# The key-value state of a linear attention block: one product of unrounded operands, or three of rounded parts

## The chip, the cores and the metric

The kernel runs on one core of one Trainium2 chip. The time is the device time of one execution in microseconds (us). Five engines matter: TensorE (PE; its weight loads are listed apart as PEld), VectorE (DVE), ScalarE (ACT), GpSimd (POOL), and SyncE (SP), which issues all DMAs here. Each engine works through its own instructions in the order in which they stand.

## The reference

One block on x of 2048 tokens by 576 columns, all float32. x is layer-normalized; then a linear attention with 32 heads of 18 columns and a gated feed-forward net (576 to 4608 to 576) are multiplied.

```python
q, k, v = qkv[0], qkv[1], qkv[2]
phi = lambda t: jnp.where(t > 0, t + 1, jnp.exp(t)) + 1e-6      # elu + 1
pq, pk = phi(q), phi(k)
kv = jnp.einsum("bhsd,bhse->bhde", pk, v)
z = jnp.einsum("bhsd->bhd", pk)
num = jnp.einsum("bhqd,bhde->bhqe", pq, kv)
den = jnp.einsum("bhqd,bhd->bhq", pq, z)[..., None] + 1e-6
o = num / den
...
s = _A_ref(xn, A_wqkv, A_wo)
g = _silu(_B_ref(xn, B_w1, B_b1, B_w2, B_b2))
return x + s * g
```

The change concerns `kv` and `z`, called the state below: sums over all tokens of value times key, and of the keys.

## The kernel before, in words

Most products on TensorE are made of rounded parts. A float32 operand is split into a high part, rounded to the type `F32R` by a copy (listed as CAST), and a low part, the difference, rounded to the same type; the product is then high·high + high·low + low·high, three products of rounded operands in place of one of unrounded ones. The state was an exception: its operands were plain float32, and each of its products was one instruction in the program.

The first stage (to about 149 us of the span) goes over 16 tiles of 128 tokens, t = 0 to 15. For each tile:

- x of the tile is made ready, transposed and split into `xh` and `xl`. Tiles 0 to 3 are normalized in rows (for 1 to 3 on ScalarE, `normalize_x`, L221), transposed on TensorE (`transpose_x`, bank `pt`) and split from the bank (L238 to L249). From tile 4 on a transposed x is loaded, centred on POOL (L276), scaled on VectorE (L279), rounded on ScalarE (L287), and the rest subtracted on VectorE (L291, L292).
- TensorE projects keys and 126 columns of values into a PSUM tile of two banks, `pk`; later the other 450 value columns into `pv`. Both come from one pool of three such tiles.
- `phi` (L339) makes elu of the keys: relu, exp and a shift on ScalarE (L328, L330, L332, tile `e`), then one VectorE instruction (L334) that reads `pk` and `e` and writes the tile `phi` in SBUF. That was the last read of the keys in `pk`.
- `copy_v` (L364) copies the values on ScalarE (L367, L369) into one of two buffers `vb`, five groups of 126 columns or fewer, each with a column of ones behind, which gives `z`.
- `state` (L373) multiplies, for the tile before, each group of values (127 columns, the weights) with the same group of keys (126 columns, in the last group 72) and adds up in two banks, `ps_kva` and `ps_kvb`, over all tiles.

So the order on TensorE is: keys of t, (transposes of x tile t+1, up to t = 2), state of t−1, values of t. The state of tile 15 stands behind the first query projection. The whole stage is recorded with a helper that holds every engine to the order of the code, so an instruction that waits holds up all behind it on its engine. In the same queues stand the statistics of later x tiles (VectorE L190 to L194) and the splits of weights for the later stages (L392 to L431). The later stages (queries, attention output, up and down projections) take the rest of the span and are not changed.

At the start POOL clears the value buffers (L149) and puts in the ones (L150), between the steps that make the identity matrix for the warm-up transposes.

Of the kernel before, what the change touches and what calls it, by code (L numbers as in the profile page):

```python
# [8 lines left out]
F32 = mybir.dt.float32  # L9
F32R = mybir.dt.float32r  # L10
U8 = mybir.dt.uint8
AF = mybir.ActivationFunctionType
ALU = mybir.AluOpType
PSUM = bass.MemoryType.PSUM

P = 128
S = 2048
D = 576
HD = 288
# [3 lines left out]
NT = S // P  # L23
# [8 lines left out]
G = 7 * DH  # L32
GROUPS = [(g, min(G, D - g)) for g in range(0, D, G)]
NG = len(GROUPS)
# [10 lines left out]
def linear_attention_gated_ffn(ctx, tc, x, xT, wqkv, wo, w1, w1e, b1, w2, b2, out):  # L45
    nc = tc.nc
    SUB, MUL, ADD = ALU.subtract, ALU.mult, ALU.add
# [34 lines left out]
    def bank2(name):  # L82
        return psum.tile([P, 2, 512], F32, tag="pp", name=name)
# [4 lines left out]
    def as2(ap):  # L88
        return ap.rearrange("p (a b) -> p a b", a=2)
# [49 lines left out]
    t1 = ph1.enter_context(tc.tile_pool(name="t1", bufs=2, side="right", reuse_waits="tile"))  # L139
    nhalf = t1.tile([P, 1], F32, name="nhalf", bufs=1)  # L140
    nc.gpsimd.memset(nhalf, -0.5)
    tiny = cst.tile([P, 1], F32, name="tiny")
# [1 line left out]

    v_bufs = [t1.tile([P, NG, P], F32, name=f"vb{i}", bufs=1) for i in range(2)]
    for v in v_bufs:
        nc.gpsimd.memset(v, 0.0)  # L149
        nc.gpsimd.memset(v[:, :, G : G + 1], 1.0)  # L150

    mask = t1.tile([P, 4 * G], U8, name="mask", bufs=1)
    mf = t1.tile([P, 7, DH], F32, name="mf", bufs=1)
# [185 lines left out]
    def phi(pool, ps, name, between=lambda: None):  # L339
        out = []  # L340
        steps = phi_steps(pool, ps, name, out)
        next(steps)
        between()
        for _ in steps:
            pass
        return out
# [17 lines left out]
    def copy_v(v, g, ps):  # L364

        n = ps.shape[1] // G
        nc.scalar.copy(v[:, g : g + n, :G], ps[:, : n * G].rearrange("p (g c) -> p g c", c=G))  # L367
        if n * G < ps.shape[1]:
            nc.scalar.copy(v[:, g + n, : ps.shape[1] - n * G], ps[:, n * G :])  # L369

    ps_kv = []

    def state(t, k_t, v_t):  # L373
        for i, (g, n) in enumerate(GROUPS):
            dst = ps_kv[0][: G + 1, g : g + n] if i < 4 else ps_kv[1][: G + 1, :n]
            nc.tensor.matmul(  # L376
                dst, v_t[:, i, : G + 1], k_t[:, g : g + n],
                start=(t == 0 and i in (0, 4)), stop=(t == NT - 1), skip_group_check=True,
            )

# [137 lines left out]
    for t in range(NT):  # L520
# [19 lines left out]
        pk = bank2(f"pk{t}")  # L540
        v_t = v_bufs[t % 2]
# [17 lines left out]
        values = lambda: copy_v(v_t, 0, pk[:, 1, HD : HD + VB])  # L559
        if t + 1 < NTR:  # L560
            if t:
                k_t, _ = phi(t1, pk, f"k{t}", values)
            transpose_x(t + 1)
            if t == 0:
                project(t, wv_h, wv_l, pv, FIRST_V[1], cols=v_cols, begin=False)
            for j in sums2:
                w2_hi(j)
            for j in sums2:
                w2_lo(j)
            if t - 1 in WE_SUMS:  # L570
                we_hi(WE_SUMS[t - 1]), we_lo(WE_SUMS[t - 1])
            if t == 0:
                layernorm(2)
            if t + 2 < NTR:
                offset(t + 2)
            if t == 0:
                k_t, _ = phi(t1, pk, f"k{t}")
        else:
            if not last:
                set_x_hi(t + 1), set_x_lo(t + 1)  # L580
            for j in sums2:
                w2_hi(j)
            for j in sums2:
                w2_lo(j)
            if t - 1 in WE_SUMS:
                we_hi(WE_SUMS[t - 1]), we_lo(WE_SUMS[t - 1])
            k_t, _ = phi(t1, pk, f"k{t}", values)
        if pend is not None:
            if not ps_kv:
                ps_kv += [bank1("ps_kva"), bank1("ps_kvb")]  # L590
# [515 lines left out]
    for i in range(1, NT + 4):  # L1106
        if 2 < i < NT:
            query(i)
        if i in X_STORES:
            at, src = X_STORES[i]  # L1110
# [461 lines left out]
    for step in range(n_chunks):  # L1572
        half, c = divmod(step, NC)
# [77 lines left out]
        for j in range(CF // 2):  # L1651
            n = 2 * step + j
# [64 lines left out]
```

## Time and profile before

| | us |
|---|---|
| median of 3 runs | 1093.29 (1093.01 to 1093.33) |
| the profiled execution, its own time | 1093.08 |
| span of its instructions | 1091.2 |
| of the span, first stage to the end of the last state | about 149 |
| busy in the first 45 to 60 us: PE, DVE, ACT, POOL (of 15) | 15.00, 12.12, 7.80, 9.86 |
| granted TensorE clock over the span | 1.00 |

In a row of the timeline stand the start, the duration, the engine, the line, the operation, the output and inputs, sizes, and in brackets how long the engine stood idle before it and what ended the wait. In a row of groups stand the count, the busy time, the mean in ns of one instruction, and the idle time before them. A product of two unrounded float32 operands appears as two records on PE and on PEld; one of rounded parts as one.

### The profile page before, as it was taken

To read this page: it belongs to the slowest core of one execution; us is meant where nothing else is said; L and a number is where in the kernel's file an instruction comes from. 1 tells how busy PE (TensorE), PEld (TensorE's weight loads), DVE (VectorE), ACT (ScalarE), POOL (GpSimd) and SP (SyncE) were. 2 spreads that over 40 slices of the span, in tenths; PEclk is the share of its full clock that TensorE was granted. 3 is DMA by queue.
4 is the path that set the end of the run, shared out by engine and by line. 5 is a ranking of instruction groups with operands and counts; after the bars stand their busy time and mean duration, and the time that the engine had idled before them with its cause. 6 is when DMAs were issued, how large, how long until landed. Compare 5 with 4: busy or idle time off the path is not lost.

```text
span 1091.2 us, 18129 instructions
## 1 busy us (share of the span) xinstructions
PE 1083.6 (99%) x6710; PEld 1007.8 (92%) x6710; DVE 794.9 (73%) x1100; ACT 548.8 (50%) x957; POOL 456.6 (42%) x391
## 2 busy tenths in 40 slices
PE   9999999999999999999999999999999999999998
PEld 8999999999898998988989989899898998988988
DVE  7766459888688898888988988657475574664856
ACT  6545466465646456465564654624335244252552
POOL 3566414332546455464555553414324143241340
PEclk9999999999999999999999999999999999999999
DMA  7997635675958658576585669968676666767352
GB/s 239 240 226 210 215 103 182 213 246 183 342 221 315 219 195 331 172 292 235 205 332 176 261 232 409 379 234 309 223 231 215 213 225 225 229 220 226 126 185 87
DMA packets 87106, 254.28 MB, mean 233 GB/s; under 512 B 11751, under 2 KB 24039, under 8 KB 84330
## 3 DMA queue, kind: packets, MB, share of 16 engines
q1 hardware_dynamic: 87018, 253.13, 68.9%
q8 instruction: 53, 0.87, 0.3%
q14 instruction: 35, 0.29, 0.1%
HBM read 156.57 MB, written 94.58 MB: 230 GB/s over the span
## 4 chain that ended last, share of the span: by engine, by line
PE 99%; DMA 0%; DVE 0%; SPq 0%; issue 0%; ACT 0%
PE pm L1349 35%; PE a L1187 16%; PE e L1187 10%; PE bc L1187 10%; PE pk L315 6%; PE pq L315 6%; PE ps_s L811 5%; PE pv L315 4%; PE pd L1465 2%; PE ps_kva L376 1%; PE ptp L793 1%; DMA w<-wqkv 0%; PE ps_kw L725 0%; PE ps_kvb L376 0%; SPq L353 0%
## 5 line engine op out<-in xcount | busy, mean ns | idle before, releaser
L1355 DVE TENSOR_TENSOR macc<-pm,macc 128x576 f32<-128x576 f32 x218 | 164.2, 753 | 56.3 <-PE pm L1349 55.8
L835 ACT CAST h_h<-g 128x512 fp32r<-128x512 f32 x204 | 122.7, 620 | 132.6 <-PE pm L1349 132.0
L838 DVE TENSOR_TENSOR h_l<-g,h_h 128x512 fp32r<-128x512 f32 x204 | 154.6, 768 | 14.8 <-ACT h_h L835 13.9
L1315 POOL TENSOR_TENSOR mid<-g 128x512 f32<-128x512 f32 x34 | 43.9, 1292 | 130.2 <-ACT g L1203 130.2
L1216 ACT COPY mid<-a 128x512 f32<-128x512 f32 x36 | 21.1, 587 | 110.5 <-PE a L1187 110.2
L1222 DVE TENSOR_TENSOR bc<-bc,mid 128x512 f32<-128x512 f32 x36 | 25.1, 697 | 52.2 <-PE bc L1187 40.7
L881 POOL TENSOR_TENSOR w1raw<-w1raw 128x256 f32<-128x256 f32 x18 | 13.2, 736 | 114.2 <-ACT h_h L835 65.6
L1309 POOL TENSOR_TENSOR g<-g 128x512 f32<-128x512 f32 x34 | 52.3, 1538 | 20.8 <-ACT h_h L835 16.7
L1235 DVE TENSOR_TENSOR z<-a,mid 128x512 f32<-128x512 f32 x36 | 25.1, 697 | 46.6 <-PE a L1187 46.6
L1437 POOL TENSOR_TENSOR fin1l<-fin1h,fin1l 128x288 f32<-128x288 f32 x8 | 7.1, 882 | 120.2 <-DMA fin1l<-s_dram 71.5
L1312 POOL TENSOR_TENSOR g<-g 128x512 f32<-128x512 f32 x34 | 52.5, 1545 | 7.6 <-DVE h_l L838 5.6
L1306 POOL TENSOR_TENSOR g<-g 128x512 f32<-128x512 f32 x34 | 50.4, 1482 | 2.7
L776 POOL TENSOR_TENSOR pbuf<-phiq,den 128x576 f32<-128x576 f32 x16 | 19.0, 1188 | 62.0 <-DVE den L775 62.0
L1225 ACT COPY mid<-a 128x512 f32<-128x512 f32 x36 | 21.1, 585 | 44.4 <-PE a L1187 44.3
L1236 ACT COPY mid<-a 128x512 f32<-128x512 f32 x36 | 21.1, 587 | 40.0 <-DVE z L1235 40.0
L838 DVE TENSOR_TENSOR h_l<-mid,h_h 128x512 fp32r<-128x512 f32 x34 | 38.1, 1120 | 2.0 <-ACT h_h L835 2.0
L315 PE MATMUL pk<-wkv_h,xh 128*128 128x288 f32 (+1 forms) x160 | 38.2, 321 | 0.5 <-DVE xh L245 0.5
L315 PE MATMUL pk<-wkv_l,xh 128*128 128x288 f32 (+1 forms) x160 | 38.5, 322 | 0.1
L811 PE MATMUL ps_s<-kw_h,th 128*128 128x288 f32 x160 | 35.3, 302 | 0.0
L315 PE MATMUL pq<-wq_h,xh 128*128 128x288 f32 x160 | 34.7, 298 | 0.0
L315 PE MATMUL pq<-wq_l,xh 128*128 128x288 f32 x160 | 34.3, 296 | 0.0
L763 POOL TENSOR_TENSOR eq<-phiq,zb 128x576 f32<-128x576 f32 x16 | 22.9, 1428 | 27.2 <-DVE kw L736 19.4
(891 smaller groups left out, 3709.5 us busy)
## 6 DMA issues: line engine op xcount, KB each, us to landing
we<-we_dram SPq DMA_DIRECT2D x36, 448.0 KB, 5.5
w2raw<-w SPq DMA_DIRECT2D x10, 1152.0 KB
w1raw<-w SPq DMA_DIRECT2D x18, 512.0 KB, 4.8
op_a<-wa SPq DMA_DIRECT2D x18, 512.0 KB, 4.7
op_c<-wc SPq DMA_DIRECT2D x18, 512.0 KB
op_d<-wd SPq DMA_DIRECT2D x18, 512.0 KB, 2.9
wc<-op_c SPq DMA_DIRECT2D x18, 512.0 KB, 6.7
wa<-op_a SPq DMA_DIRECT2D x18, 512.0 KB, 4.5
```

The costliest lines, as they stand in the source:

```text
L315: nc.tensor.matmul(ps[:, h, : ws.stop - ws.start], st, w[:, k, ws], start=(begin and i == 0), stop=(end and i == len(seq) - 1), skip_group ...
L811: nc.tensor.matmul(ps[:, h, :HD], st[:, k, :], w[:, k, h * HD : (h + 1) * HD], start=(i == 0), stop=(i == len(seq) - 1),)
L835: nc.scalar.copy(pair[0], src)
L838: eng.tensor_tensor(pair[1], src, pair[0].bitcast(F32), op=SUB)
L1187: nc.tensor.matmul(ps, st, mv, start=first and n == 0, stop=n == len(seq) - 1, skip_group_check=True,)
L1222: tt(B, B, m1_sb, op=ADD)
L1306: tt(src[5, pr], A(1, 0), A(1, 1), op=ADD)
L1309: tt(src[6, pr], src[5, pr], A(0, 0), op=SUB)
L1312: tt(src[3, pr], A(0, 1), src[6, pr], op=SUB)
L1315: tt(src[7, pr], A(0, 0), A(1, 0), op=SUB)
L1349: nc.tensor.matmul(ps[:, q, :HD], hs[p][st][:, cs], m[:, p, :], start=(n == 0 and i not in CHAIN), stop=(n == 5), skip_group_check=True,)
L1355: nc.vector.tensor_tensor(dst, src, dst, op=ADD)
```

## The change

Values and keys get a high and a low part, and the state becomes three products per group.

- The value buffers hold two parts, `[P, 2, NG, P]` in place of `[P, NG, P]`. `copy_v` rounds the values on ScalarE into part 0 and then subtracts on VectorE into part 1, reading the bank again. The ones are in part 0 and zeros in part 1.
- `phi_key` takes the place of `phi` for the keys. VectorE writes elu back into `pk`, in place; ScalarE rounds it from there into part 0 of a new tile `kk`, and VectorE subtracts part 0 from the bank into part 1.
- `state` runs fifteen products a tile, high·high, high·low and low·high for each of five groups.

Per tile that is one more ScalarE instruction (the cast of the keys), and on VectorE one subtraction for the keys and three for the values. No instruction is taken away, and no DMA is changed.

```diff
-    v_bufs = [t1.tile([P, NG, P], F32, name=f"vb{i}", bufs=1) for i in range(2)]
+    v_bufs = [t1.tile([P, 2, NG, P], F32R, name=f"vb{i}", bufs=1) for i in range(2)]
     for v in v_bufs:
-        nc.gpsimd.memset(v, 0.0)
-        nc.gpsimd.memset(v[:, :, G : G + 1], 1.0)
+        nc.gpsimd.memset(v.bitcast(F32), 0.0)
+        nc.gpsimd.memset(v[:, 0, :, G : G + 1].bitcast(F32), 1.0)
...
     def copy_v(v, g, ps):
         n = ps.shape[1] // G
-        nc.scalar.copy(v[:, g : g + n, :G], ps[:, : n * G].rearrange("p (g c) -> p g c", c=G))
+        parts = [(v[:, :, g : g + n, :G], ps[:, : n * G].rearrange("p (g c) -> p g c", c=G))]
         if n * G < ps.shape[1]:
-            nc.scalar.copy(v[:, g + n, : ps.shape[1] - n * G], ps[:, n * G :])
+            parts.append((v[:, :, g + n, : ps.shape[1] - n * G], ps[:, n * G :]))
+        for dst, src in parts:
+            nc.scalar.copy(dst[:, 0], src)
+        for dst, src in parts:
+            nc.vector.tensor_tensor(dst[:, 1], src, dst[:, 0].bitcast(F32), op=SUB)
+
+    def phi_key(ps, name, between=lambda: None):
+        e = t1.tile([P, D], F32, tag="e", name=f"e{name}")
+        kk = t1.tile([P, 2, D], F32R, tag="kk", name=f"kk{name}")
+        src = ps[:, :, :HD]
+        nc.scalar.activation(as2(e), src, AF.Relu, scale=-1.0)
+        between()
+        nc.scalar.activation(e, e, AF.Exp, scale=-1.0)
+        nc.scalar.activation(e, e, AF.Identity, bias=tiny[:, 0:1])
+        nc.vector.scalar_tensor_tensor(src, src, 1.000001, as2(e), op0=ADD, op1=ALU.max)
+        nc.scalar.copy(as2(kk[:, 0]), src)
+        nc.vector.tensor_tensor(as2(kk[:, 1]), src, as2(kk[:, 0]).bitcast(F32), op=SUB)
+        return kk
...
     def state(t, k_t, v_t):
         for i, (g, n) in enumerate(GROUPS):
             dst = ps_kv[0][: G + 1, g : g + n] if i < 4 else ps_kv[1][: G + 1, :n]
-            nc.tensor.matmul(
-                dst, v_t[:, i, : G + 1], k_t[:, g : g + n],
-                start=(t == 0 and i in (0, 4)), stop=(t == NT - 1), skip_group_check=True,
-            )
+            for j, (a, b) in enumerate(((0, 0), (0, 1), (1, 0))):
+                nc.tensor.matmul(
+                    dst, v_t[:, a, i, : G + 1], k_t[:, b, g : g + n],
+                    start=(t == 0 and i in (0, 4) and j == 0), stop=(t == NT - 1 and j == 2),
+                    skip_group_check=True,
+                )
...
-                k_t, _ = phi(t1, pk, f"k{t}", values)
+                k_t = phi_key(pk, f"k{t}", values)
```

The last replacement stands in all three places where the stage calls `phi` for keys; in tile 0 `phi` and now `phi_key` stand without `values`, whose copies come from `pv` later.

The new instructions stand in two queues at places where others wait. First ScalarE in tile 0, from the transposed x tile 1 (`pt1b`) to the first activation of tile 1's keys; `ek` is the tile `e` of the keys, `vb` a value buffer, `xn` the normalized x tile 2, `kkk` the tile `kk`. Before:

```order
L242 CAST xh_82<-pt1b 128x128
L328 ACTIVATE ek_307<-pk_216 128x576
L330 ACTIVATE ek_307<-ek_307 128x576
L332 ACTIVATE ek_307<-ek_307,tiny 128x576
L367 COPY vb_115<-pv_259 128x3x126
L367 COPY vb_115<-pv_259 128x126
L369 COPY vb_115<-pv_259 128x72
L221 ACTIVATE xn_316<-x_199,mv_302 128x576
L221 ACTIVATE xn_316<-x_199,mv_302 128x64
```

and now, with the engines that each instruction waits for:

```order
L242 CAST xh_82<-pt1b 128x128 [waits PE_49]
L380 ACTIVATE ek_307<-pk_216 128x576
L382 ACTIVATE ek_307<-ek_307 128x576 [waits Activation_49]
L383 ACTIVATE ek_307<-ek_307,tiny 128x576 [waits Activation_49]
L385 CAST kkk_308<-pk_216 128x576 [waits DVE_49]
L371 CAST vb_115<-pv_259 128x3x126 [waits PE_49]
L371 CAST vb_115<-pv_259 128x126 [waits DVE_49]
L371 CAST vb_115<-pv_259 128x72
L221 ACTIVATE xn_321<-x_199,mv_302 128x576 [waits DMAHW5_49,Pool_49]
L221 ACTIVATE xn_321<-x_199,mv_302 128x64
```

The cast of the keys, which waits for VectorE, is now ahead of the values' copies and of the normalization of x tile 2, and the second copy waits for VectorE too.

Second VectorE in a tile of the steady part, tile 4: from the scaling of x tile 5 (`xt`) to the statistics of a later one. Before:

```order
L279 TENSOR_TENSOR xt_441<-xt_441,bc_443 128x640
L291 TENSOR_TENSOR xl_85<-xt_441,xh_84 128x4x128
L292 TENSOR_TENSOR xh_84<-xt_441,xh_84 64x128
L431 TENSOR_TENSOR w1h<-w1u,w1h 128x896
L334 SCALAR_TENSOR_TENSOR phik_681<-pk_642,ek_676 128x576
L190 BN_STATS st_714<-x_536 128x6
```

and now:

```order
L279 TENSOR_TENSOR xt_461<-xt_461,bc_463 128x640 [waits DMAHW6_49,DMAHW5_49,Pool_49]
L291 TENSOR_TENSOR xl_85<-xt_461,xh_84 128x4x128 [waits Activation_49]
L292 TENSOR_TENSOR xh_84<-xt_461,xh_84 64x128
L451 TENSOR_TENSOR w1h<-w1u,w1h 128x896 [waits DMAHW1_49,Activation_49]
L373 TENSOR_TENSOR vb_115<-pk_692,vb_115 128x126 [waits PE_49,Activation_49]
L384 SCALAR_TENSOR_TENSOR pk_692<-pk_692,ek_726 128x2x288 [waits DVE_49,Activation_49]
L386 TENSOR_TENSOR kkk_727<-pk_692,kkk_727 128x576 [waits Activation_49]
L373 TENSOR_TENSOR vb_115<-pv_751,vb_115 128x3x126 [waits PE_49,Activation_49]
L373 TENSOR_TENSOR vb_115<-pv_751,vb_115 128x72
L190 BN_STATS st_779<-x_571 128x6 [waits DMAHW3_49]
```

The elu instruction has a value subtraction ahead of it and three subtractions behind it, of which the first waits for the cast of the keys and the second for the values of `pv`; the statistics and the scaling of the next x tile come after them.

More of the change, by code (lines that the diff above doesn't have):

```diff
@@ L576, in linear_attention_gated_ffn @@
             if t == 0:
-                k_t, _ = phi(t1, pk, f"k{t}")
+                k_t = phi_key(pk, f"k{t}")
         else:
@@ L586, in linear_attention_gated_ffn @@
                 we_hi(WE_SUMS[t - 1]), we_lo(WE_SUMS[t - 1])
-            k_t, _ = phi(t1, pk, f"k{t}", values)
+            k_t = phi_key(pk, f"k{t}", values)
         if pend is not None:
```

## The prediction

> **What bounds the kernel now.** I read the page's busy shares and its chain of waits first, then the timeline of TensorE around one token tile of the first stage, where the change lies.
>
> ```profile
> span 1091.2 us, 18129 instructions
> PE 1083.6 (99%) x6710; PEld 1007.8 (92%) x6710; DVE 794.9 (73%) x1100; ACT 548.8 (50%) x957; POOL 456.6 (42%) x391
> PE 99%; DMA 0%; DVE 0%; SPq 0%; issue 0%; ACT 0%
> ```
>
> TensorE is busy for 99% of the span and holds 99% of the chain that ended last: what TensorE is given more or less, the kernel gains or loses in full, and other engines matter only where they make it stand. The next view is the timeline of TensorE over tiles 3 and 4 of the first stage (start, duration, engine, line, operation, count).
>
> ```profile
> 39.18 1.05 PE L376 MATMUL ps_kva<-phik,vb 128*127 128x126 f32 x8
> 40.06 0.34 PE L376 MATMUL ps_kvb<-phik,vb 128*127 128x72 f32 x2
> 40.20 0.45 PE L315 MATMUL pv<-wkv_h,xh 128*128 128x450 f32 x1
> 40.49 0.36 PE L315 MATMUL pv<-wkv_l,xh 128*128 128x450 f32 x1
> 40.70 0.37 PE L315 MATMUL pv<-wkv_h,xl 128*128 128x450 f32 x1
> 43.16 0.48 PE L315 MATMUL pk<-wkv_h,xh 128*128 128x288 f32 x2
> 47.63 1.04 PE L376 MATMUL ps_kva<-phik,vb 128*127 128x126 f32 x8
> ```
>
> No row has an idle time in brackets: TensorE goes from state to values to keys without a stop, one tile every 47.63 − 39.18 = 8.45 us. A five-product state stands as ten records, since each product of unrounded operands is two, each with its own weight load. Its share: from 39.18 to the second pv product at 40.49, less one pv product (40.70 − 40.49 = 0.21), is 1.10 us, so 0.11 us a record. The 72-column records are no cheaper: (40.49 − 0.21 − 40.06) / 2 = 0.11. [...]
>
> **The change, part by part.**
>
> *State products on TensorE.* Five products of two records become fifteen products of rounded operands. Are those one record, and at which pace? The last down-projection has the narrowest rounded products of the trace in a row:
>
> ```profile
> 1085.14 0.50 PE L1465 MATMUL pd<-w__11186,hp 128*128 128x192 f32 x3
> 1085.47 0.50 PE L1465 MATMUL pd<-w__11206,hp 128*128 128x192 f32 x3
> 1085.81 0.50 PE L1465 MATMUL pd<-w__11222,hp 128*128 128x192 f32 x3
> ```
>
> Three products (one record each) take 0.33 to 0.34 us, 0.11 us each, though at the pace of the 450-column products (0.21 us, so 0.46 ns a column) 192 columns would need 0.09. [...] So a state takes 15 × 0.111 = 1.66 us in place of 1.10: +0.55 us, times 16 tiles = **+8.9 us**. Bounds: if only streaming counted, 126 and 72 columns need 0.057 and 0.033 us, a state 3 × (4 × 0.057 + 0.033) = 0.79 us, or −5.0 us in all; if each product took 0.115, +10.0 us. I take 0.111, which two kinds of row give.
>
> [...]
>
> *The keys in tiles 0 and 1.* What is new on ScalarE and VectorE is a queue order. ScalarE rounds the keys (cast) only after VectorE has written elu back to the bank; everything behind that cast on ScalarE waits. Here are the rows of ScalarE, VectorE and TensorE there, before:
>
> ```profile
> 17.98 0.78 ACT L332 ACTIVATE ek<-ek,tiny 128x576 f32<-128x576 f32 x1
> 18.67 0.62 ACT L367 COPY vb<-pv 128x378 f32<-128x378 f32 x2
> 19.18 0.23 ACT L369 COPY vb<-pv 128x72 f32<-128x72 f32 x1
> 19.70 1.20 ACT L221 ACTIVATE xn<-x,mv 128x576 f32<-128x576 f32 x2 [0.29 <-DVE mv L209]
> 23.45 0.67 ACT L238 CAST xh<-pt 128x640 fp32r<-128x640 f32 x1
> ...
> 19.69 0.76 DVE L334 SCALAR_TENSOR_TENSOR phik<-pk,ek 128x576 f32<-128x576 f32 x1
> 23.85 0.76 DVE L334 SCALAR_TENSOR_TENSOR phik<-pk,ek 128x576 f32<-128x576 f32 x1
> ...
> 21.15 0.71 PE L232 MATMUL pt<-ident,xn 128*128 128x128 f32 x5
> 25.67 0.49 PE L315 MATMUL pk<-wkv_h,xh 128*128 128x288 f32 x2
> ```
>
> and the prices of the new operations, from the groups by shape of the first 165 us:
>
> ```profile
> L334 DVE SCALAR_TENSOR_TENSOR phik<-pk,ek 128x576 f32<-128x576 f32 x16 | 12.1, 757 | 25.2 <-ACT ek L332 25.2
> L734 ACT COPY kw<-ps_kw 126x576 f32<-126x576 f32 x2 | 1.3, 639 | 1.5 <-PE ps_kw L725 1.5
> L246 DVE TENSOR_TENSOR xl<-pt,xh 128x512 fp32r<-128x512 f32 x2 | 1.4, 680 | 0.0
> L246 DVE TENSOR_TENSOR xl<-pt0a,xh 128x256 fp32r<-128x256 f32 x2 | 0.8, 424 | 0.1
> ```
>
> A cast of the keys is 0.64 us on ScalarE (a copy of the same size out of PSUM), the keys' subtraction 0.76 us on VectorE (its 576-column operation with one operand in PSUM), and the values' subtractions, at 1 ns a column and 0.17 us fixed (from 680 and 424), 0.55, 0.29 and 0.24 us for 378, 126 and 72 columns. Writing elu into PSUM instead of SBUF has no row; I take the same 757 ns, and bound it by 0 and +0.3.
>
> Tile 0, step by step: elu of keys 0 ends at 19.69 + 0.76 = 20.45. Cast: to 21.1. ScalarE's copy of the first 378 value columns: to 21.5. VectorE subtracts keys to 21.9, then those values to 22.4, and ScalarE's next copy (126 columns) waits for that subtraction, as its row in the order shows: to 22.7, the 72 columns to 22.9. Only then comes the normalization of x tile 2 (before at 19.70, 1.20 us for its two pieces), to about 24.0. TensorE wants it for the transposes at 21.15, and can start them on the first piece at about 23.65: **+2.5 us**, nothing else being ahead of them on TensorE. The state of tile 0, the values and the keys behind them go down by the same. The range is 1.8 (elu 0 earlier, no hand-off times) to 3.3 (each of seven hand-offs 0.1 dearer).
>
> Tile 1: VectorE's three statistics took from 20.45 to 23.85, 3.4 us with the hand-offs; now they begin at about 23.2, end at 26.7, elu of keys 1 ends at 27.7 (its value subtraction of 0.29 first), the cast at 28.35, and the cast of x tile 2 (0.67, before at 23.45), which now stands behind it, at 29.0. The keys of tile 2 want it at 25.67 + 2.5 + 0.55 = 28.7, so TensorE waits **+0.4 us** (bounds 0 and 1). The x tile after it, the last that ScalarE normalizes, has room: VectorE stood 4 us before the elu of keys 2, which the same delays fill first.
>
> ```profile
> 32.59 0.76 DVE L334 SCALAR_TENSOR_TENSOR phik<-pk,ek 128x576 f32<-128x576 f32 x1 [4.09 <-ACT ek L332]
> ```
>
> *VectorE in the later tiles.* New there: 0.76 for keys, 1.08 for values, and a wait of about 0.74 for the key cast; less 0.08 for each overlap at a start, 2.24 us a tile. The heaviest tile of the trace:
>
> ```profile
> 44.89:52.58 7.69, 7.69 (x50) 7.45 (x49) 6.77 (x10) 4.33 (x8) 4.45 (x3) 1.00 0.96 216
> 77.27:85.72 8.45, 8.45 (x54) 8.21 (x53) 6.25 (x11) 4.43 (x9) 6.54 (x6) 1.00 1.03 244
> ...
> 46.51 1.73 DVE L291 TENSOR_TENSOR xl<-xt,xh 128x512 fp32r<-128x512 f32 x1 [0.79 <-ACT xh L287]
> 83.84 0.76 DVE L334 SCALAR_TENSOR_TENSOR phik<-pk,ek 128x576 f32<-128x576 f32 x1 [1.25 <-ACT ek L332]
> ```
>
> From one scaling of x to the next (third column of busy times is VectorE) it needs 7.69 us with one wait of 0.79 for ScalarE's rounding of x, and 9.93 with the new work, against a TensorE tile of 8.45 + 0.55 = 9.00: it falls 0.9 us behind. The second window, without its wait of 1.25, comes to 7.2 + 2.24 = 9.44. Lighter tiles give it back. What it may lose: a value subtraction must end before the state one key projection later.
>
> ```profile
> 43.35 0.48 ACT L367 COPY vb<-pv 128x378 f32<-128x378 f32 x1 [0.91 <-PE pv L315]
> 43.72 0.23 ACT L369 COPY vb<-pv 128x72 f32<-128x72 f32 x1
> ```
>
> The copies end at 43.95, the subtractions 0.79 later at 44.7, the state comes at 47.63: 2.9 us of cover. I count **0**; with the cover gone, each of the ten tiles 3 to 12 costs 0.9, less the 2.9 of cover, +6 us at most.
>
> *The start.* POOL clears twice the width of the value buffers, 0.63 us more before the identity that the warm-up transposes need. They and the first keys come up to 0.6 us later, but the value weights behind them wait for DMA anyway:
>
> ```profile
> 1.00 0.63 POOL L149 MEMSET vb<- 128x640 f32 x1
> 2.02 4.03 PE L363 MATMUL warm<-ident 128*128 128x128 f32 x20 [2.02 <-POOL ident masks.py:199]
> 10.72 3.69 ACT L357 CAST wkv_h<-raw_v 128x576 fp32r<-128x576 f32 x5 [0.84 <-DMA raw_v<-wqkv]
> ```
>
> I count 0 (bounds 0 and 0.6). The sum: +8.9 + 2.5 + 0.4 = +11.8 us, on the profiled execution's 1093.08 (span 1091.2): 1104.9. The median of the runs is 0.2 above that execution, so I forecast **1105.1 us**.
>
> **The rivals.**
> (a) *VectorE becomes the bound.* The 9.93 against 9.00 repeats over the middle tiles and the cover is used up: +11.8 plus up to 6, 1107 to 1111, say 1109. For it speak the two windows above; against it VectorE's idle times before L334, 25.2 us over the sixteen tiles.
> (b) *Weights load ahead.* With a fifteen-long run of narrow loads the pace falls halfway between streaming (0.053 on average) and 0.111, 0.082 us: a state 1.23 us, +2.1 us in all, with +2.9 for the start 1098.1. The rows of 192 columns, twelve in a run, speak against it. [...]
> (c) *Faster.* Loads hidden wholly, 0.79 us a state: −5.0 + 2.9 = −2.1, 1091. It decides below a pace of (1.10 − 2.9 / 16) / 15 = 0.061 us a product. Even then VectorE's 9.93 would hold a tile above 8.45 for a while. Nothing in the rows reaches that pace.
> (d) *The change does not do what it says:* products of rounded parts below some width between 126 and 192 columns cost two records too. Thirty records of 0.111 are 3.33 us a state: +35.6 + 2.9, 1131.8.
> (e) *No stop at the start:* the normalization comes in time after all, +8.9 alone, 1102.
>
> **How the numbers follow.** Forecast 0.60, (a) 0.22, (b) 0.05, (c) 0.03, (d) 0.02, (e) 0.08. The range takes in (e), most of (a), and the bounds of the load price (+8.0 at 0.1075 us to +10.0) with those of the start: 1100 to 1112. A measurement of this kernel tells about 0.2%, 2.2 us, from no change. Faster by that needs less than 1091.1, (c) at its end: 0.02. Within it the rest of (c) and a little of (b): 0.03. Slower: 0.95.
>
> **What would show it.** In the changed profile a state should be fifteen records, 1.66 us from its first start to the values' start less their first lead; TensorE should show one idle time of about 2 us before the transposes of tile 2, released by ScalarE's normalization at L221, and under 0.5 before the keys of tile 2; no state should wait on VectorE's subtractions. The forecast is wrong if the products' starts stand 0.06 or 0.08 us apart, or if states in the middle tiles wait for VectorE.

## The result, and the profile after

| | before | changed |
|---|---|---|
| median, us | 1093.15 (1092.89 to 1093.33, 4 runs) | 1112.59 (1111.43 to 1113.17, 4 runs) |
| the profiled execution, its own time | 1093.08 | 1111.43 |
| span of its instructions | 1091.2 | 1109.3 |

The ratio is 1.0177, with a 95% interval of 1.0163 to 1.019: the kernel is slower by 19.4 us. I had forecast 1105.1, and the range to 1112 just misses the median. The profiled execution is the shortest of the four, with a mean granted clock of 0.998; the other three show 0.995, which matters further down.

First the page's head and its chain of waits:

```profile
span 1109.3 us, 18400 instructions
PE 1095.5 (99%) x6790; PEld 1018.1 (92%) x6790; DVE 824.5 (74%) x1164; ACT 557.3 (50%) x973; POOL 459.1 (41%) x391
PE 90%; DVE 5%; issue 2%; DMA 2%; ACT 1%; SPq 0%; POOL 0%; DVEq 0%
```

TensorE has 80 records more (16 tiles of 15 in place of 10) and 11.9 us more of busy time. But it now holds 90% of the chain where it held 99%: VectorE has 5%. The waits of TensorE, by what ended them (us in total, times, longest), say where:

```profile
PE warm L363 <- POOL ident masks.py:199: 2.5, 1, 2.5
PE pt L232 <- ACT xn L221: 2.3, 1, 2.3
PE ps_kva L395 <- ACT kkk L385: 1.6, 2, 1.4
PE ps_kva L395 <- DVE kkk L386: 1.3, 3, 0.5
PE pk L315 <- DVE kkk L386: 0.5, 1, 0.5
PE pk L315 <- DVE xh L245: 0.5, 1, 0.5
```

The first row is the wait for the identity matrix, 2.0 us before the change. The second and the fifth row are the two stops at the start, where the forecast has them. The third and fourth, 2.9 us of the state waiting for the keys' cast and subtraction, should not be there. The timeline of TensorE shows both, and between them a state in a tile without a stop:

```profile
24.03 0.77 PE L232 MATMUL pt<-ident,xn 128*128 128x128 f32 x5 [2.31 <-ACT xn L221]
29.85 0.55 PE L315 MATMUL pk<-wkv_h,xh 128*128 128x288 f32 x2 [0.52 <-DVE kkk L386]
...
52.98 1.44 PE L395 MATMUL ps_kva<-kkk,vb 128*127 128x126 f32 x12
54.26 0.47 PE L395 MATMUL ps_kvb<-kkk,vb 128*127 128x72 f32 x3
54.56 0.45 PE L315 MATMUL pv<-wkv_h,xh 128*128 128x450 f32 x1
54.84 0.36 PE L315 MATMUL pv<-wkv_l,xh 128*128 128x450 f32 x1
...
80.02 0.22 PE L395 MATMUL ps_kva<-kkk,vb 128*127 128x126 f32 x1
80.63 1.45 PE L395 MATMUL ps_kva<-kkk,vb 128*127 128x126 f32 x11 [0.39 <-DVE kkk L386]
89.66 1.44 PE L395 MATMUL ps_kva<-kkk,vb 128*127 128x126 f32 x12
108.83 1.44 PE L395 MATMUL ps_kva<-kkk,vb 128*127 128x126 f32 x12
119.43 0.33 PE L395 MATMUL ps_kva<-kkk,vb 128*127 128x126 f32 x1 [1.44 <-ACT kkk L385]
```

The state from 52.98 to 54.84, less one value product of 0.21, takes 1.65 us: 15 × 0.110. From tile 2 to tile 6 the states begin 9.01 us apart, as forecast. From the state of tile 6 on (80.02, then 89.66, 99.00, 108.83, 119.43 and 130.80) they come late: 9.64, 9.34, 9.83, 10.60 and 11.37 us apart, 5.73 more than five times 9.01, and then 9.01 again, from tile 11 on, where no statistics of later x tiles are left to make.

In the last of these steps there is something else as well. This is a window of 3.41 us in it (busy times of PE, PEld, DVE, ACT and POOL; the third number from the end is the granted TensorE clock):

```profile
122.14:125.55 3.41, 3.41 (x11) 3.02 (x10) 2.41 (x3) 3.20 (x6) 1.65 (x1) 0.50 0.48 164
```

TensorE had half its clock there, shortly behind a stop of 1.44 us ahead of the state and one of 0.47 behind its first product. Of the kernel before, the profiled execution shows none of this: its clock is 1.00 from 5.40 to 1090.84 us, all but the first and the last microseconds.

So there are two candidates for what the forecast left out, VectorE in the middle tiles and the clock, and in the median they make up some 7 us between them.

### The profile page after: what moved, and what is told of

The parts are those of the page before. It is cut to its first block, busy times and chain, and to the rows that moved or that the text cites. A ratio compares the mean times of both kernels' runs of the same rounds, so it can differ in the third digit from the quotient of the medians.

```text
span 1109.3 us, 18400 instructions
## 1 busy us (share of the span) xinstructions
PE 1095.5 (99%) x6790; PEld 1018.1 (92%) x6790; DVE 824.5 (74%) x1164; ACT 557.3 (50%) x973; POOL 459.1 (41%) x391
## 4 chain that ended last, share of the span: by engine, by line
PE 90%; DVE 5%; issue 2%; DMA 2%; ACT 1%; SPq 0%; POOL 0%; DVEq 0%
PE pm L1369 34%; PE a L1207 16%; PE bc L1207 10%; PE e L1207 10%; PE pq L315 5%; PE ps_s L831 5%; PE pd L1485 2%; PE pk L315 2%; PE pv L315 2%; PE ptp L813 1%; PE ps_kva L395 1%; DVE xh L292 1%; DVE pk L384 1%; DVE vb L373 1%; DMA x<-x 1%
## 5 line engine op out<-in xcount | busy, mean ns | idle before, releaser
L195 POOL TENSOR_TENSOR mv<-mv,nhalf 128x1 f32<-128x1 f32 x16 | 13.7, 854 | 53.3 <-DVE mv L194 53.3
```

## The experiments

All were timed in three rounds beside the kernel before, whose median was 1093.34 us for the first four below, 1093.18 for "The stop filled alone" and 1093.13 for the other four. So a difference between runs of different groups is not sure to 0.2 us.

### The products alone

The state takes its fifteen rounded products, but VectorE's elu writes the rounded keys straight into `kk` as it did before, and the low parts are zeros that nobody computes: no cast, no subtraction. The low parts are so left out of the result.

```diff
...
-        nc.vector.scalar_tensor_tensor(src, src, 1.000001, as2(e), op0=ADD, op1=ALU.max)
-        nc.scalar.copy(as2(kk[:, 0]), src)
-        nc.vector.tensor_tensor(as2(kk[:, 1]), src, as2(kk[:, 0]).bitcast(F32), op=SUB)
+        nc.vector.scalar_tensor_tensor(as2(kk), src, 1.000001, as2(e), op0=ADD, op1=ALU.max)
...
-                    dst, v_t[:, a, i, : G + 1], k_t[:, b, g : g + n],
+                    dst, v_t[:, a, i, : G + 1], (k_zero if b else k_t)[:, g : g + n],
```

> Only TensorE's part of the change: fifteen rounded products a state, but no low parts are made (VectorE's elu writes the rounded keys straight to SBUF, the low parts are zero tiles), so the cast of the keys and the four subtractions are left out; the output lacks the low parts' share. Theory 'three causes' (the weight load sets the products' pace; a stop at the start; VectorE falls behind): the loads alone, 16 x 0.56 = +9.0 us and some tenths for the longer clearing at the start, 1102.3 us (1101.5 to 1103.2), no wait of TensorE in the middle tiles, clock 1.00. Rival 'TensorE alone' (the narrow rounded products or the clock cost the whole +19): 1107 or more.

Measured: 1102.24 us (1102.08 to 1102.73), ratio 1.0083 (1.0066 to 1.0099). That is +8.9 us, the term of the forecast; that it is so to the tenth is luck, as the four runs spread over 0.65 us. The states stand 9.01 us apart from tile 2 to the end, and TensorE waits for nothing but what it waited for before.

### The other engines' work alone

The new work of ScalarE and VectorE is all there, in plain float32; the state runs its five unrounded products as before.

```diff
...
-            for j, (a, b) in enumerate(((0, 0), (0, 1), (1, 0))):
+            for j, (a, b) in enumerate(((0, 0),)):
...
```

> The other part: the copies, the elu written back, the cast's place in ScalarE's queue and the four subtractions as in the change, in plain float32, and five unrounded products a state as before. Theory 'three causes': the stop at the start stays (+2.8), and VectorE, which takes 9.58 us a tile over tiles 3 to 10 whatever TensorE does, now faces tiles of 8.45: cover of 2.9 gone after three tiles, then 1.1 a tile for six or seven, so +10 to +12, 1103 to 1106 us: as dear as in the whole change less about 7, the parts do not add. Rival 'the parts add': 1093.2 + 2.8 + 4.0 + 1.7 of clock = 1101.7 or less. Rival 'TensorE alone': 1096.

Measured: 1106.19 us (1105.72 to 1106.86), ratio 1.0118 (1.0103 to 1.0133), 0.2 above the range expected, and far from both rivals. The products cost 8.9 alone and this costs 12.9 alone; together they cost 19.4, not 21.8. That is what one expects if a wait is left: TensorE's shorter tile of 8.45 us only waits longer for the same VectorE. TensorE's waits in this kernel, but for those of its first microseconds:

```profile
PE pk L315 <- DVE xl L291: 3.1, 6, 0.8
PE pt L232 <- ACT xn L221: 2.3, 1, 2.3
PE ps_kva L395 <- ACT kkk L385: 1.9, 3, 1.5
```

The same stop of 2.3 us at the start, with five products in place of fifteen, and the keys waiting for VectorE's split of x (L291) in six tiles. Its profiled execution has a mean granted clock of 0.998, as that of the change with its one stretch of half clock.

### Normalizing x tile 2 ahead of the keys of tile 0

If the normalization at L221 is late because it stands behind the cast of the keys on ScalarE, it can stand ahead of the keys' activations.

```diff
             if t == 0:
+                normalize_x(2)
                 k_t = phi_key(pk, f"k{t}")
...
-        if t + 2 < NTR:
+        if 0 < t < NTR - 2:
             normalize_x(t + 2)
```

> The change with one line moved: in tile 0 the normalization of x tile 2 stands ahead of the elu and cast of keys 0 in ScalarE's queue. Both theories: the stop of 2.3 us before the transposes goes. Theory 'VectorE paces the middle': VectorE's own chain starts no earlier, so TensorE meets it sooner and the gain is mostly given back in tiles 6 to 10: 1111.5 to 1112.6. Rival 'the stop is on the path to the end': 1110.2.

Measured: 1114.7 us (1113.6 to 1116.08), ratio 1.0196 (1.018 to 1.0211): a miss, slower than the change itself. Two rows of ScalarE's timeline:

```profile
19.98 1.20 ACT L221 ACTIVATE xn<-x,mv 128x576 f32<-128x576 f32 x2 [3.02 <-DVE mv L209]
21.09 0.63 ACT L380 ACTIVATE ek<-pk 128x576 f32<-128x576 f32 x1
```

and the transposes in TensorE's:

```profile
25.64 1.00 PE L232 MATMUL pt<-ident,xn 128*128 128x128 f32 x5 [4.04 <-DVE kkk L386]
```

The normalization needs VectorE's statistics of that tile (L209), so ScalarE stood for 3.0 us and the keys' activations came after. And the transposes have a second thing to wait for: their bank `pt` is the one that the keys of tile 0 held, out of a pool of three, and it comes free with the last read of those keys. Before, that was the elu; now it is the subtraction. The stop grew from 2.3 to 4.0 us, and half clock followed it: twelve products of the state behind it, from 26.29 to 28.88 us, stand 0.22 us apart, where the change has 0.11, and the clock over the run is 0.995.

### GpSimd quiet

GpSimd's centring of x and its sums over weights are left out (so is their part of the result). VectorE's instructions are untouched.

```diff
...
-        if NTR <= t + 2 < NT:
-            center(t + 2)
...
-        for j in W2_SUMS.get(t, ()):
-            w2_sum(j)
-        if t in WE_SUMS:
-            we_sums(WE_SUMS[t])
```

> The change without GpSimd's centring of x and its sums of weights in the first stage (left out: the mean is not subtracted from x tiles 4 to 15, and the sums of weights are wrong). Theory 'contention': VectorE's L291 (1.73 us in every tile now) and L292 (1.42 in every second) fall to 0.69 and 0.29 when GpSimd does nothing beside them, VectorE's tile falls from 9.58 to about 8.0, under TensorE's 9.01; the states' waits in tiles 6 to 10 and the clock's drop behind them vanish: 1093.2 + 9.0 + 2.9 + 0.4 = 1105.5 (1104.5 to 1106.5). Rival 'VectorE's new work itself': durations stay, 1112.

Measured: 1107.8 us in the median (1105.19 to 1108.04), ratio 1.0126 (1.0111 to 1.0142). Here is why this bears on VectorE. In the changed kernel VectorE and GpSimd stand like this, in the tile from 72 us on:

```profile
72.11 0.83 DVE L279 TENSOR_TENSOR xt<-xt,bc 128x640 f32<-128x640 f32 x1
73.73 1.73 DVE L291 TENSOR_TENSOR xl<-xt,xh 128x512 fp32r<-128x512 f32 x1 [0.79 <-ACT xh L287]
75.50 1.42 DVE L292 TENSOR_TENSOR xh<-xt,xh 64x128 fp32r<-64x128 f32 x1
79.81 0.76 DVE L386 TENSOR_TENSOR kkk<-pk,kkk 128x576 fp32r<-128x576 f32 x1 [0.71 <-ACT kkk L385]
82.28 0.83 DVE L279 TENSOR_TENSOR xt<-xt,bc 128x640 f32<-128x640 f32 x1
```

GpSimd over the same stretch:

```profile
72.24 1.11 POOL L195 TENSOR_TENSOR mv<-mv,nhalf 128x1 f32<-128x1 f32 x1 [3.51 <-DVE mv L194]
73.32 1.60 POOL L276 TENSOR_TENSOR xt<-xt,bc 128x640 f32<-128x640 f32 x1
74.87 1.90 POOL L412 TENSOR_TENSOR w2r<-w2r 128x576 f32<-128x576 f32 x1
```

L291 starts while GpSimd centres x (L276, to 74.92) and ends 0.54 us after it; L292 starts while GpSimd sums weights (L412, to 76.77) and ends 0.15 after it. With GpSimd quiet the same L291 reads:

```profile
64.15 0.69 DVE L291 TENSOR_TENSOR xl<-xt,xh 128x512 fp32r<-128x512 f32 x1 [0.79 <-ACT xh L287]
```

0.69 us in every tile, and L292 0.29. No wait of TensorE is left in the middle tiles, whose states stand 9.01 us apart. So it is VectorE that holds up the states in the changed kernel, and what makes it slow enough to do so is GpSimd beside it. One more such meeting stands ahead of the longest wait of the states: the split of weights at 115.27 us (L451) took 2.37 us beside two instructions of GpSimd, where it takes 1.09 alone, and the state at 119.43 waited 1.44.

L291 and L292 of the changed kernel end each some 0.15 us sooner than GpSimd's end plus VectorE's own time alone (0.69 and 0.29 us) would give. By what means GpSimd holds VectorE up the runs don't show.

The time was not 1105 in every run, though. The run with a granted clock of 0.999 took 1105.19; the others, at 0.996 and 0.997, took 1107.71 to 1108.04. In the profiled one of these the stop of 2.3 us at the start is TensorE's only wait behind the first products, and a clock of 0.997 is some 3.3 us lost of 1106.

### VectorE's waits filled

Now with all the work in place. From tile 3 on, the statistics of a later x tile (`stats_of`) stand between the elu and the keys' subtraction, where VectorE waits 0.71 us for the cast, and the operations on weight sums stand ahead of the split of x, where it waits 0.79.

```diff
...
         nc.scalar.copy(as2(kk[:, 0]), src)
+        gap()
         nc.vector.tensor_tensor(as2(kk[:, 1]), src, as2(kk[:, 0]).bitcast(F32), op=SUB)
...
-            if not last:
-                set_x_hi(t + 1), set_x_lo(t + 1)
             for j in sums2:
                 w2_hi(j)
...
-            k_t = phi_key(pk, f"k{t}", values)
+            if not last:
+                set_x_hi(t + 1), set_x_lo(t + 1)
+            k_t = phi_key(pk, f"k{t}", values, stats_of)
```

> The changed kernel with VectorE's two remaining waits in a tile filled: from tile 3 on the statistics of the tile five ahead stand between the elu's write-back and the subtraction of the keys (where VectorE waits 0.71 us for ScalarE's cast), and the four operations on the weight sums stand ahead of the operations on x (where it waits 0.79 us). The work is the same. Theory (VectorE's tile of 9.0 and 10.16 us in turn, 9.58 on the mean, is what holds the states back in tiles 6 to 11): VectorE's tile falls by 0.7 to 1.5 us, to some 8.1 to 8.9, below TensorE's 9.01; the states follow one another in 9.01 us from tile 3 to the end, no wait of TensorE on the keys' cast or subtraction stays in tiles 6 to 11, and the time is 1105.2 us with the clock at full speed throughout, or about 2.6 us more (1107.8) where the stop of 2.3 us before the transposes of tile 2 brings half clock as it did with GpSimd's work left out. Rival (the loss of the middle tiles is contention for its own sake, or ScalarE's chain): no gain, 1111 to 1113. Rival (the statistics, now later, come too late for GpSimd and the normalization): a new wait at the transposes in each tile, 1113 to 1120.

Measured: 1108.68 us (1108.4 to 1108.86), ratio 1.0141 (1.0126 to 1.0156), 0.9 above the 1107.8 worked out for a run with half clock. The waits of TensorE in the middle tiles are gone and every state from tile 2 on comes 9.01 us after the last. One caution on how: the new order also parts VectorE from GpSimd.

```profile
62.91 2.01 DVE L421 TENSOR_TENSOR w2o<-w2r,w2o 128x576 fp32r<-128x576 f32 x1
64.84 0.68 DVE L291 TENSOR_TENSOR xl<-xt,xh 128x512 fp32r<-128x512 f32 x1
65.55 0.29 DVE L292 TENSOR_TENSOR xh<-xt,xh 64x128 fp32r<-64x128 f32 x1
```

L291 and L292 are down to 0.68 and 0.29; the subtraction of weight sums (L421) now stands beside the centring and takes 2.01 us instead of 0.91. Nor are the waits all gone: from 40 to 120 us those ahead of L291 and the keys' subtraction fell from 12.0 to 0.8 us, but a new one, 5.3 in all, came ahead of the split of weights, which waits for ScalarE there. How much of the gain came from the filled waits and how much from the smaller overlap, the run doesn't tell.

What it still has is the start. TensorE's row of the transposes:

```profile
24.44 0.76 PE L232 MATMUL pt<-ident,xn 128*128 128x128 f32 x5 [2.30 <-ACT xn L221]
```

and the window from shortly behind it, with the clock at 0.50:

```profile
25.72:32.55 6.83, 6.83 (x24) 6.26 (x24) 4.49 (x13) 2.28 (x4) 2.96 (x7) 0.50 0.47 21
```

### The same, with TensorE kept busy in the stop at the start

Twenty more transposes of the identity stand on TensorE ahead of the transposes of x tile 2. They compute nothing that is read.

```diff
+            if t == 1:
+                again = bank1("warm2")
+                for _ in range(NWARM):
+                    nc.tensor.transpose(again[:, :P], ident, ident)
             transpose_x(t + 1)
```

> The kernel of the run before this one (VectorE's waits filled) with 20 more transposes of the identity on TensorE, written to a bank of their own that nobody reads, ahead of the transposes of x tile 2, where TensorE stands still for 2.3 us. At 0.108 us each they take 2.2 us, so they fill the stop and add nothing by themselves. Theory (it is the stop on TensorE that brings the stretches of half clock): the granted clock stays at 0.999 or 1.0 in every run, no half clock follows tile 2, and the time is 1105.2 to 1105.6 us, some 2.5 below the run before this one where that one shows half clock. Rival (half clock has another cause, such as the load of TensorE or the time since the start): the same clocks and the same time as without them, 1107 to 1108.

Measured: 1105.85 us (1105.51 to 1106.15), ratio 1.0116 (1.0101 to 1.0131), 0.25 above the range expected: 2.8 us faster for twenty instructions of no use. TensorE's rows:

```profile
21.87 2.35 PE L590 MATMUL warm<-ident 128*128 128x128 f32 x20
24.34 0.77 PE L232 MATMUL pt<-ident,xn 128*128 128x128 f32 x5
```

and the same window as above:

```profile
25.72:32.55 6.83, 6.32 (x39) 5.76 (x38) 5.79 (x17) 3.89 (x8) 2.87 (x7) 1.00 0.51 25
```

The useful work begins at the same moment (24.34 against 24.44), but at full clock: 39 records of products in the window against 24. All four runs are at 0.999 or 1.0, all four of the run without the transposes at 0.995 to 0.997. That this stop brings the half clock is so shown, not argued.

The 6.83 us at half clock without them are twice the 3.41 of the change. A stop of 2.3 us was enough in this execution, and 1.44 with 0.47 in that of the change.

### VectorE's waits filled, and the normalization in ScalarE's gap

Where ScalarE waits 1.7 us for VectorE's elu of the keys of tile 0, ahead of the cast, it can normalize x tile 2.

```diff
...
         nc.vector.scalar_tensor_tensor(src, src, 1.000001, as2(e), op0=ADD, op1=ALU.max)
+        mid()
         nc.scalar.copy(as2(kk[:, 0]), src)
...
-                k_t = phi_key(pk, f"k{t}")
+                k_t = phi_key(pk, f"k{t}", mid=lambda: normalize_x(2))
...
-        if t + 2 < NTR:
+        if 0 < t < NTR - 2:
             normalize_x(t + 2)
```

> VectorE's waits filled as in e5, and ScalarE's normalization of x tile 2 put between the elu's write-back and the cast of the keys of tile 0, where ScalarE waits 1.7 us for VectorE. Theory: the transposes of tile 2 then wait for the bank of the keys of tile 0 alone, which VectorE's subtraction frees at about 22.6 us; the stop falls from 2.3 to about 1.1 us, it is too short to bring half clock, and the time is 1103.9 to 1104.5 us. Rival (as with the normalization ahead of all of the keys' work: it waits for VectorE's offset of tile 2, and the keys' cast behind it is late): the stop stays at 2.3 us or grows to 3, and the time is 1107 to 1111.

Measured: 1108.52 us (1107.24 to 1108.76), ratio 1.0138 (1.0123 to 1.0153): a miss. The stop at the transposes did fall to 1.0 us, as expected, yet no time was won:

```profile
PE pk L315 <- DVE kkk L388: 2.1, 1, 2.1
PE pt L232 <- DVE kkk L388: 1.0, 1, 1.0
PE pk L315 <- DVE xl L291: 1.0, 1, 1.0
```

The keys of tile 2 now wait 2.1 us where they waited 0.5, so the two stops come to 3.1 us instead of 2.8: TensorE only came sooner to the next thing that VectorE had not done. VectorE has three statistics and the elu and subtraction of the keys of tile 1 between, and its subtraction ends at the same time as in the change:

```profile
28.93 0.76 DVE L388 TENSOR_TENSOR kkk<-pk,kkk 128x576 fp32r<-128x576 f32 x1 [0.70 <-ACT kkk L386]
```

In the change it began at 28.94. So the start's loss is VectorE's queue, wherever TensorE meets it. In the profiled execution half clock followed behind the second stop: the pairs of key products from 30.58 us on stand 0.58 us apart, where they stand 0.32 apart at full clock, and the mean clock from 20 to 40 us is 0.91, which makes 3.6 us at half. That a stop of 1.1 us is too short to bring it was my estimate, and this run leaves it open. The one run at a clock of 1.0 took 1107.24, with the third row's 1.0 us (a wait that ends at 123.9 us) still in it, if it was there as in the profile.

### The stop filled alone

The change as it is, with only the twenty transposes of the run above.

> The changed kernel as it is, with nothing but the 20 transposes of the identity on TensorE ahead of the transposes of x tile 2 (as in e6), so that it does not stand still there. VectorE's order is that of the change. Theory (the loss beyond the products is made of three: the late start, which stays; VectorE's tile of 9.0 and 10.16 us in turn, which stays; half clock after the stop at the start, which goes): the time is that of e6, 1105.85, plus what VectorE's waits in tiles 6 to 11 cost, worked out at about 4.1 us from the state starts of the changed kernel (0.64 + 0.32 + 0.82 + 1.60 + 2.36 = 5.74, less some 1.6 for the 3.41 us at half clock among them): 1109.5 to 1110.3, with the waits on the keys' cast and subtraction in tiles 6 to 11 still there, and half clock, if any, only behind those. Rival (the changed kernel's half clock comes from these middle waits, and the stop at the start has none in it): the time stays at 1112 to 1113.

Measured: 1109.6 us in the median (1108.53 to 1112.06), ratio 1.0146 (1.0129 to 1.0163). Two runs at a clock of 0.999 took 1108.53 and 1108.55; the other two, at 0.998 and 0.997, 1110.65 and 1112.06. The profiled one is the 1112.06, and its half clock lies behind the middle stops (1.4 us for the cast, 0.5 for the subtraction) now:

```profile
119.56:126.38 6.82, 6.82 (x26) 6.33 (x26) 5.07 (x8) 3.36 (x6) 1.57 (x1) 0.50 0.48 153
```

No run lies in the range expected, 1109.5 to 1110.3; that the median of two pairs does is luck. The median fell by 3.0 us with the stop filled, and the half clock of the profiled execution comes behind the later stops. The two runs at full clock give VectorE's price by itself: 1108.54 − 1105.85 = 2.7 us, less than the 4.1 that I had read from the profiled execution of the change. Part of that difference may be chance, though neither run at full clock was profiled: in the profiled execution of the change, VectorE's split of weights at 40.00 us took 2.13 us, in the profiled one of this run 1.32, and left VectorE 0.9 us further ahead.

### High parts only

The state from the high parts alone: five rounded products, nothing to subtract. The low parts are left out, and the state carries the rounding of values and keys.

```diff
...
-            for j, (a, b) in enumerate(((0, 0), (0, 1), (1, 0))):
+            for j, (a, b) in enumerate(((0, 0),)):
                 nc.tensor.matmul(
-                    dst, v_t[:, a, i, : G + 1], k_t[:, b, g : g + n],
+                    dst, v_t[:, a, i, : G + 1], k_t[:, g : g + n],
```

> The state from five products of rounded parts only, high part of the values by high part of the keys: the low parts of values and keys, and the ten products with them, are left out, so the state carries the rounding of both. VectorE's elu writes the rounded keys at once; no cast, no subtractions. Theory (a rounded product runs at its weight load, 0.111 us, and an unrounded one at two of them): a state takes five products, 0.555 us in place of 1.105 before, 0.55 us less in each of 16 tiles: 1093.3 - 8.8 = 1084.5 us, at full clock, with state starts 7.9 to 8.0 us apart in the middle tiles. Rival (a rounded product alone has a cost of its own, or VectorE's and ScalarE's chain then sets the pace at 8.4 to 8.5 us a tile): no gain, 1090 to 1094.

Measured: 1084.61 us (1084.22 to 1084.83), ratio 0.9922 (0.9906 to 0.9939): 8.5 us faster than the kernel before, against 8.8 worked out.

```profile
61.89 0.55 PE L391 MATMUL ps_kva<-kkk,vb 128*127 128x126 f32 x4
62.28 0.25 PE L391 MATMUL ps_kvb<-kkk,vb 128*127 128x72 f32 x1
62.36 0.45 PE L315 MATMUL pv<-wkv_h,xh 128*128 128x450 f32 x1
62.66 0.36 PE L315 MATMUL pv<-wkv_l,xh 128*128 128x450 f32 x1
```

From 61.89 to 62.66, less a value product of 0.21, is 0.56 us: 0.11 a product, the same with five in a run as with fifteen. It is faster than both kernels, at the price of the low parts. Of the kernels that make the low parts and multiply all three products none came below 1105.

## Why the prediction was wrong, step by step

The forecast's sum was +11.8 us; the median came out at +19.4. The runs split that, each term to some 0.2 us, as they come from different groups:

| term | forecast | measured | from |
|---|---|---|---|
| products on TensorE | +8.9 | +8.9 | the products alone, 1102.24 against 1093.34 |
| the start | +2.9 | +3.6 | stop and waits filled, 1105.85, less the products alone |
| VectorE in the later tiles | 0 | +2.7 | the stop filled alone at full clock, 1108.54, less 1105.85 |
| half clock behind stops, and chance in VectorE's waits | none | +4.1 | the change, 1112.59, less 1108.54 |

**State products on TensorE: right.** One record a product, 0.11 us at 126 columns as at 72; forecast 1.66 us a state, measured 1.65. That the weight load sets this pace was my estimate, from the pace being the same at both widths. No run shows it: every load in these products has 127 or 128 columns, so a fixed cost of each product would look the same. By its own figures the term is 9.0 (1.66 less 1.10, times 16), and its bound at 0.1075 us a product +8.2, not +8.0; neither moves anything.

**The keys in tiles 0 and 1: right in place, and in cause for the first of two.** The transposes waited 2.31 us for L221 (forecast 2.5 for the delay). The keys of tile 2 waited 0.52 us (forecast 0.4, though its own figures, 29.0 less 28.7, give 0.3), and not for the cast of x tile 2 but for the bank that the keys of tile 1 held until their subtraction (L386). This second hold, of a bank by the subtraction, was missing from my working; at the transposes it came first in the change (the subtraction of tile 0's keys ended at 22.34, the transposes began at 24.03), and only the run with the normalization first showed it as the last to end.

**The start: counted 0, and a part of it came through.** The value buffers' clearing takes 1.16 us in place of 0.63, and the keys of tile 1 began at 16.97 in place of 16.56. It was within its bounds of 0 to 0.6, and with the two stops (2.31 and 0.52) it makes 3.2 of the 3.6.

**VectorE in the later tiles: wrong. This is the step that failed first.** I wrote that the heaviest tile falls 0.9 us behind and that "lighter tiles give it back", and counted 0. There were no lighter tiles. The windows from one scaling of x to the next, of two tiles in a row, in the changed kernel (third busy time: VectorE):

```profile
63.12:72.11 8.99, 8.99 (x59) 8.74 (x58) 7.25 (x14) 4.50 (x9) 5.41 (x6) 1.00 0.72 219
72.11:82.28 10.17, 9.78 (x65) 9.32 (x63) 8.43 (x14) 4.77 (x9) 4.53 (x3) 1.00 0.61 213
```

VectorE needs 8.99 and 10.17 us in turn, in both of them with only its two waits of 0.7 and 0.8 us for ScalarE: 9.58 on the mean against TensorE's 9.01. My own two windows came to 9.93 and 9.44, both over 9.00; I had the loss in hand and waved it off. The argument against rival (a), 25.2 us of idle time ahead of the elu over sixteen tiles, was also too weak as it stood: that is 1.6 us a tile, and the new work of 2.24 less TensorE's 0.55 asks for 1.7. With 9.58 the bound of the forecast gives 10 × 0.57 − 2.9 = 2.8 us, and 2.7 were measured. That this fits so well is partly luck. VectorE's scalings of x from 43.97 to 120.69 us bound eight such tiles, not ten. And the cover of 2.9 us was that of the values' subtractions, while what the states waited for was the keys' cast and subtraction: that of tile 4 ended at 61.41, 0.6 us ahead of its state at 61.99, and that of tile 6 at 80.57, 0.55 behind its state's start at 80.02.

What my windows could not show is why all tiles became heavy. Before, VectorE had slack, and whether L291 met GpSimd's centring changed from tile to tile: 1.73 us at 46.51, but

```profile
61.99 0.69 DVE L291 TENSOR_TENSOR xl<-xt,xh 128x512 fp32r<-128x512 f32 x1 [0.80 <-ACT xh L287]
```

Its mean over the middle tiles (40 to 120 us) was 1.03 us before (first row), and 1.73 after:

```profile
L291 DVE TENSOR_TENSOR xl<-xt,xh 128x512 fp32r<-128x512 f32 x10 | 10.3, 1029 | 11.6 <-ACT xh L287 11.6
L291 DVE TENSOR_TENSOR xl<-xt,xh 128x512 fp32r<-128x512 f32 x8 | 13.8, 1726 | 6.4 <-ACT xh L287 6.4
```

Once VectorE is the late one, GpSimd waits for its statistics (3.51 us in the row above) and then always starts its centring just ahead of VectorE's split of the next tile. As I read the rows, the two fall into step, and the collision that came now and then comes in every tile.

**Half clock: not in the forecast at all.** The kernel before had no stop on TensorE after the first 7 us, and so nothing in its trace showed that a stop costs more than its length. The forecast priced each stop at its length alone. Here the stop at the start was followed by two stretches of 3.41 us at half clock with the waits filled, and the later stops by one in the change and by two with the stop filled alone. The pair behind the stop at the start cost 2.8 us (1108.68 against 1105.85). How the 4.1 us of the last row divide between these stretches and VectorE's varying luck can be estimated from the granted clock. The three executions at 0.995 lost 0.005 × 1110 = 5.5 us of clock, 0.4 of it at the very end as in the profiled one, which leaves about 5.1: three stretches of 3.41 us at half clock, 1.7 each. (The 0.998 of the profiled one gives 2.2, its one stretch and the end.) So in the median the row is half clock in the main. The profiled execution has one stretch, at most 1.7 of the 2.9 us by which its 1111.43 lies above 1108.54.

The clock records of the change's trace also say something of when a stop brings it. Half clock begins 34 stretches of 3.413 us after full clock was first granted (from 6.08 to 122.14 us) and lasts one more. So how a stop falls on this grid may count. Of the 3.41 us just ahead TensorE was busy for 2.24; with the waits filled, it was busy for 1.28 of the 3.41 ahead of 25.72, from the transposes at 24.44 on. The stop at the start of the change fell across a point of the grid (23.15 us), with TensorE busy for 1.98 us of the stretch ahead of it and 2.53 of the one behind, and no half clock came. The limit stays open: 1.98 us came without half clock and 2.24 with it.

**The rivals.** (a) was right in kind. Its price of 1109 is near the 1108.54 that the change takes with the clock held at full, but partly by luck: it gave VectorE 4 us where 2.7 were measured, and the start 0.7 too little. At the clock as it was, the median lies above its range of 1107 to 1111. (b) and (c), loads hidden, and (d), two records, fall with the 0.11 us; (e) falls with the 2.31.

## What to carry to other kernels

When work is added to an engine that was not the bound, compare its new time per step with the bound's in every window you have: if the mean is over, no lighter step will give it back, and what you found on one engine's rows was measured with slack that the change takes away. Collisions between two engines that come now and then can come in every step once one of them waits for the other, as here VectorE's split of x went from 1.03 us on the mean to 1.73. And a stop on TensorE can cost more than its length: filling a stop of 2.3 us with useless products took 2.8 us off the time here.

## What the runs showed of the hardware

- A stop on TensorE of 2.3 us can be followed by half its clock (0.50 in the windows): with the waits filled it was, for 6.83 us from 25.72 on. So was a stop of 1.4 us with one of 0.5 in two executions, for 3.41 us in the change and for 6.82 with the stop filled alone. With the waits and the stop at the start filled, four runs of four had a clock of 0.999 or 1.0. The same stop did not bring it in every execution: the profiled one of the change had 1.00 from 6.08 to 122.14 us. There half clock began 34 times 3.413 us after full clock was first granted, and TensorE had been busy for 2.24 us of the 3.41 just ahead; with the waits filled it had been busy for 1.28.
- VectorE's subtraction of 512 columns (L291) took 0.69 us alone and 1.73 beside GpSimd's centring, and the small one of 128 columns (L292) 0.29 alone and 1.42 beside GpSimd's sum of weights: beside GpSimd each ended 0.15 to 0.54 us after GpSimd's instruction.
